# RWKV-6 recurrence and MLP on one core: round 0 loaded in rows of three steps, level 0 masked by AND, one MLP step moved between outputs and level products

## The chip, the cores and the metric

The kernel runs on one core of a Trainium2 chip. The core has a matrix engine (TensorE, called PE in the profile; its weight loads are listed apart as PEld), a vector engine (VectorE, DVE), a scalar engine (ScalarE, ACT), GpSimd (POOL), and a queue engine (SyncE, SP) that here only issues transfers. Each engine runs its own instructions in order and waits on semaphores for the others. Transfers run on 16 DMA engines; most are issued from SP's queue, a few from ACT's. The metric is the device time of one execution in microseconds (us). The times come from six executions, one of them with the profiler on.

## The reference

Four batches, eight heads, 768 steps, head size 48, all in float32. First a recurrence with a decaying state for each batch and head, then an MLP over the joined heads:

```python
for t in range(S):                       # S = 768, state is D x D per (batch, head), D = 48
    cur   = (u * k[t]) outer v[t]
    y[t]  = r[t] @ (state + cur)
    state = w[t][:, None] * state + k[t] outer v[t]
x  = y with heads joined                 # (4, 768, 384)
xn = (x - mean) / sqrt(var + 1e-6) * g_ln
out = x + relu(xn @ w_ch1) @ w_ch2       # 384 -> 1536 -> 384
```

## The kernel before

**Tiling.** The work is cut into 8 rounds, one for each batch and half of the sequence (384 steps). A round has two units of four heads each. A unit's `w`, `k`, `r` are loaded with one step per partition (`load`, line 122): three transfers of 128 steps for each tensor, in runs of 48 floats (192 bytes), into the tiles `nat_w`, `nat_k`, `nat_r`, where a head takes 64 columns, the last 16 of them zeros. `turned` (line 289) transposes them on PE, two heads at a time, in three blocks of 128 steps, into PSUM, and ACT copies the result into `wT` or `rkT`, so that head dimensions lie on partitions and steps along the free axis.

**The recurrence by levels.** Steps are grouped in chunks of 64. In a chunk the product between step s and a later step t carries the decays between them. This is done in six levels, lev = 0 to 5, for distances of 2^lev: `quads` (line 385) multiplies k by the odd halves of r for all chunks into PSUM (`a_ps`; 24 small products of each unit), `grow` (line 405, DVE) multiplies r and k in place by the decays of that level, and `keep` (line 422, DVE) copies from PSUM, by a mask, those elements of `a_ps` into the matrix `A` that belong to this level. `quads` of one level needs `grow` of the level before; `grow` must wait until `quads` has read. After the levels `ends`, `states`, `exchanged`, `own_outputs` and `outputs` form the chunk's state updates (`kn`, `kv`, `s`, `sx`) and the results y, and `own_term` adds the term with u. The sums of that term are made in rounds 0 and 1 by `product_sums` (line 359, small PE products with a selector, `own_ps`).

**The MLP.** `mlp(rnd)` (line 601) is a generator for one round: 12 steps of three products 128x128 by 128x384 (`h_ps`), then 12 steps of the second layer (`o_ps`). A step is six PE matmuls in the profile, since a float32 product is two passes there. The weights arrive as raw float32 and are rewritten once by ACT and DVE (`fetch`, `begin`, `shifted`, `added`, lines 217 to 273: four raw buffers, each begin asks for the next fetch).

**The order.** It is written out by hand: every engine runs its instructions in program order. First comes a prologue with round 0 (lines 695 to 777), in which `warm(n)` issues matmuls on zeros (tile `idle`) between the steps, and then a loop over rounds 1 to 8 and levels (lines 788 to 894). A slot of that loop (one round, one level) issues for an older round `states` in levels 0 and 1 and `outputs` in levels 2 and 3, then `quads`, `grow` and `keep` of the round itself, and then `fill` (line 658) mixes the other tasks (transposes for the next round and the like) with MLP steps, up to a count given by `UNTIL`. From round 3 on, the `y` products of `outputs` are thus followed at once by the `a_ps` products of `quads`:

```python
            elif old and lev < 2 * U:
                (states if lev < U else outputs)(old[lev % U])
            for q in now:
                if slot:
                    quads(q, lev)
```

PE's instructions come from memory as well: the profile lists the transfers of instructions as queues of their own (q8 and q14).

Of the kernel before, what the change touches and what calls it, by code (L numbers as in the profile page):

```python
# [12 lines left out]
I32 = mybir.dt.int32  # L13
# [39 lines left out]
def kernel(  # L53
# [68 lines left out]
    def load(q, which="wkr", eng=SP):  # L122
        for nm in which:
            for c in range(TT):
                eng.dma_start(
                    out=nat[nm][q % 2][:, c, :, 0:D],
                    in_=steps({"w": w, "k": k, "r": r}[nm], q, c),
                )

    def load_v(q, eng=SP):  # L130
        vn[q] = p4.tile([P, TT, NH, D], F32, tag="v", name=f"v{q}")
        for c in range(TT):
            eng.dma_start(out=vn[q][:, c], in_=steps(v, q, c))
# [9 lines left out]
            )  # L143


    load(0, "w", SPO)
    load(0, "r", ACT)
    load(0, "k", SPO)
    load(1, "wrk", SPO)

    sel = const.tile([P, H // 2, 2], F32, name="sel")
    POOL.memset(sel, 0.0)
# [12 lines left out]
    DVE.memset(eps, 1e-6)  # L165

    ACT.activation(out=const.tile([P, 1], F32, name="root"), in_=eps, func=AF.Sqrt)
    for nm in "wkr":
        for t in nat[nm]:
            POOL.memset(t[:, :, :, D:HP], 0.0)  # L170


    a_bufs = [const.tile([P, 2, U, NK, C], F32, name=f"A{i}") for i in range(2)]
# [5 lines left out]
    for lev in range(NLEV - 1):  # L179
        n = 1 << lev  # L180
        m = const.tile([P, C // n, n], I8, name=f"mask2_{lev}")
        POOL.memset(m, 1.0)
        for base, sign in ((0, 1), (n - 1, -1)):
            POOL.affine_select(
                out=m, in_=m, compare_op=ALU.is_ge, fill=0.0, base=base,
                pattern=[[-2 * n * sign, C // n], [0, n]], channel_multiplier=sign,
            )
        half = const.tile([P, C // 2], I8, name=f"mask{lev}")
        m = m.rearrange("p q n -> p (q n)")
        for i in range(2):  # L190
            rows = ds(C * i, C)
            POOL.tensor_copy(out=half[rows], in_=m[rows, ds(C // 2 * i, C // 2)])
        masks.append(half.rearrange("p (q n) -> p q n", n=n))

# [78 lines left out]
    def warm(n, tag="m"):  # L275

        while n > 0:
            m = min(n, RN // P)
            ps = (ps_m if tag == "m" else ps_t).tile([P, RN], F32, tag=tag, name="idle")
            PE.matmul(  # L280
                ps[:, 0 : m * P], nought.broadcast_to([P, P]), nought.broadcast_to([P, m * P]),
                start=True, stop=True,
            )
            n -= m
# [4 lines left out]
    def turned(q, nm, pr):  # L289
        a = st.setdefault(q, {})  # L290
        if pr == 0:
            if nm == "w":
                if q % U == 0:
                    st["w"] = p1.tile([P, U, W], F32, tag="w", name=f"wT{q // U}")
                a["w"] = st["w"][:, q % U]
            elif "rk" not in a:

                rk = a["rk"] = p4.tile([P, 2, W], F32, tag="rkT", name=f"rkT{q}")
                a["r"], a["k"] = rk[:, 0], rk[:, 1]
        ps = ps_t.tile([P, RN], F32, tag="t", name=f"{nm}_ps{q}_{pr}")  # L300
        for c in range(TT):
            PE.transpose(
                ps[:, ts(c, P)],
                nat[nm][q % 2][:, c, ts(pr, 2)].rearrange("p j d -> p (j d)"), ident,
            )
        ACT.copy(out=a[nm][:, ts(pr, RN)], in_=ps)
# [115 lines left out]
    def keep(rnd, lev):  # L422
        n = 1 << lev
        A, ps = a_bufs[rnd % 2], a_ps[rnd]
        if lev == NLEV - 1:
            for j in range(2):
                for i in range(2):
                    rows = ds(C * i, n)
                    late.append((A[rows, j, :, :, n:], ps[rows, j]))
        else:  # L430
            DVE.copy_predicated(
                out=A.rearrange("s j u k (q two n) -> s j (u k) q two n", two=2, n=n)[:, :, :, :, 1],
                mask=masks[lev][:, None, None].broadcast_to([P, 2, U * NK, C // (2 * n), n]),
                data=ps.rearrange("s j u k (q n) -> s j (u k) q n", n=n),
            )
        if lev == NLEV - 1:
            for q in units_of(rnd):

                a = st[q]
                a["rx"] = p2.tile([P, NK, C], F32, tag="rx", name=f"rx{q}")  # L440
                R = a["r"].rearrange("p (k i t) -> p k i t", i=2, t=C)
                for j in range(2):
                    late.append((a["rx"][ds(HP * (1 - j), HP)], R[ds(HP * j, HP), :, 1, :]))
# [232 lines left out]
    def each(f, *ranges):  # L676
        calls = [()]
        for r_ in ranges:
            calls = [c + (x,) for c in calls for x in r_]
        return [lambda c=c: f(*c) for c in calls]  # L680
# [17 lines left out]
    for nm in "wrk":  # L698
        run(each(turned, [u0], nm, pairs))
        warm(2)  # L700
    products(u0)
    quads(u0, 0)
    load(new[0], eng=SPO)
    grow(u0, 0)
    run(each(turned, [u1], "w", pairs))
    totals(0, DVE)
# [2 lines left out]
    for nm in "rk":  # L709
        run(each(turned, [u1], nm, pairs))  # L710
        warm(2)
    products(u1)
    quads(u1, 0)
    fetch(2)
# [11 lines left out]
    for lev in range(1, NLEV):  # L726
        quads(u0, lev)
        quads(u1, lev)
        run(ahead[2 * lev - 2 : 2 * lev] if lev < NLEV - 1 else [])
        if lev in (3, 4):  # L730
            begin()
        warm(3 if lev < NLEV - 1 else 0)
        for which in ("rk",) if lev < NLEV - 1 else "kr":
            for q in (u0, u1):
                grow(q, lev, which)
        keep(0, lev)
# [30 lines left out]
    quads(new[0], 0)  # L767
    quads(new[1], 0)
    warm(3)
    product_sums(new[0])  # L770
    warm(3)
    norm(0)
    begin()
    join()
# [13 lines left out]
    for rnd in range(1, NR + 1):  # L788
# [3 lines left out]
        for lev in range(NLEV):  # L792
            slot = (rnd - 1) * NLEV + lev
            if rnd == 2:

                for q in old if lev < 2 else []:
                    (states, outputs)[lev](q)
                if lev < 2:
                    mlp_step()
            elif old and lev < 2 * U:  # L800
                (states if lev < U else outputs)(old[lev % U])
            for q in now:
                if slot:
                    quads(q, lev)
# [8 lines left out]
            if rnd == 1:  # L813
                if lev < 2:
                    tasks += each(load, new, "kr"[lev], [SPO])
                if lev == 2:
                    SPO.dma_start(
                        out=u_bc,
                        in_=bass.AP(
                            tensor=u.tensor, offset=u.offset, ap=[[0, P], [D, H], [1, D]]  # L820
                        ),
                    )
                    tasks += each(load_v, now, [SPO])
                if lev == 3:
                    tasks += each(load_vx, now, [SPO])
                if lev == 1:
                    tasks += each(product_sums, now[1:])
                if lev in (4, 5):
                    own_term(now[lev - 4], POOL)
            if rnd == 2 and lev == 0:  # L830
# [96 lines left out]
```

## Time and profile before

| what | value |
|---|---|
| median of six executions | 591.06 us (589.32 to 594.54) |
| the profiled execution | 594.54 us, the slowest of the six |
| its span, first to last instruction | 592.5 us, so 2.04 us lie outside |
| granted TensorE clock, mean | 0.991 |
| PE busy | 569.9 us, 96% |
| DVE, ACT, POOL busy | 280.1, 194.8, 90.1 us |
| moved by DMA | 36.52 MB |

A share of busy time is an average over stages: the first 100 us (round 0, weights) have other limits than the rest, so each stage is read by itself, by its chain of waits and by the time in which PE has nothing running. "Issue" in the chain is time in which an engine stood still and waited for nothing that the profile shows. Groups such as `a_ps<-rkT` name the tile written and the tiles read.

### The profile page before, as it was taken

The page shows a single profiled execution, that of the slowest core. Times are in us where ns is not written, and L with a number is a line of the kernel's source. Part 1 is how long each engine was busy: PE and PEld are TensorE (multiplying, and loading weights), DVE is VectorE, ACT ScalarE, POOL GpSimd, SP SyncE. Part 2 cuts the span into 40 slices and gives each one's busy share as a digit, 9 for nine tenths or more (in the row PEclk, how much of TensorE's full clock was granted, in tenths as well). Part 3 has the DMA queues.
Part 4 walks back from the last instruction along what each step waited for, and adds up shares of the span by engine and source line. Part 5 has one row for each costly group of instructions (what it writes and reads, how often), then busy time and mean ns, then how long its engine had stood idle before and what let it go on. Part 6 is the DMA issues. An engine that isn't in the chain of part 4 may idle for free.

```text
span 592.5 us, 19009 instructions
## 1 busy us (share of the span) xinstructions
PE 569.9 (96%) x8538; PEld 382.1 (64%) x8538; DVE 280.1 (47%) x575; ACT 194.8 (33%) x426; POOL 90.1 (15%) x117
## 2 busy tenths in 40 slices
PE   8899989999999999889999899999999999999997
PEld 5676756666676766666666666667666666666554
DVE  4887999687282635424273335426245431130000
ACT  3576786313442224311433115321241015301200
POOL 6040011104430035000440007100230000000000
PEclk9998999999998999999999999999999999999999
DMA  9967885037304311340203402012000000000000
GB/s 146 189 167 167 206 232 120 12 80 137 72 16 99 65 34 23 67 81 24 54 5 74 83 14 55 2 32 59 16 1 3 14 29 2 1 15 27 0 14 27
DMA packets 120528, 36.52 MB, mean 62 GB/s; under 512 B 114176, under 2 KB 117376, under 8 KB 120448
## 3 DMA queue, kind: packets, MB, share of 16 engines
q1 hardware_dynamic: 118048, 35.01, 27.3%
q8 instruction: 67, 1.10, 0.8%
q10 hardware_dynamic: 2400, 0.30, 0.5%
q14 instruction: 13, 0.11, 0.1%
HBM read 28.51 MB, written 4.72 MB: 56 GB/s over the span
## 4 chain that ended last, share of the span: by engine, by line
PE 87%; ACT 5%; issue 2%; DVE 2%; DMA 2%; SPq 1%; ACTq 0%; DVEq 0%
PE o_ps L49 32%; PE h_ps L49 29%; PE a_ps L49 11%; PE y L49 4%; PE kv L49 2%; PE k_ps L49 2%; PE kn_ps L49 2%; PE w_ps L49 2%; PE xT_ps L49 1%; ACT rest L49 1%; PE r_ps L49 1%; ACT w_sb L49 1%; DMA nat_r<-in_r_dram 1%; PE idle L49 1%; DMA nat_k<-in_k_dram 1%
## 5 line engine op out<-in xcount | busy, mean ns | idle before, releaser
L49 PE MATMUL o_ps<-w_sb,h 128*128 128x384 f32 x576 | 200.7, 495 | 0.8 <-ACT h L49 0.8
L49 PE MATMUL h_ps<-xT,w_sb 128*128 128x384 f32 x576 | 198.2, 492 | 0.0
L49 PEld LDWEIGHTS o_ps<-w_sb,h 128*128 128x128 f32 x576 | 106.0, 193 | 63.1 <-issue 2.0
L49 PEld LDWEIGHTS h_ps<-xT,w_sb 128*128 128x128 f32 x576 | 105.7, 191 | 62.7 <-issue 0.6
L49 ACT ACTIVATE h<-h_ps 128x384 f32<-128x384 f32 x96 | 46.8, 488 | 143.2 <-PE h_ps L49 143.0
L49 PEld LDWEIGHTS a_ps<-rkT 48*64 48x64 f32 x4608 | 73.8, 135 | 23.8 <-issue 16.4
L49 DVE TENSOR_TENSOR rkT<-rkT,tot 128x768 f32<-128x768 f32 (+1 forms) x96 | 77.4, 844 | 21.3 <-PE a_ps L49 12.6
L49 PE MATMUL a_ps<-rkT 48*64 48x32 f32 x4608 | 79.0, 220 | 8.2 <-issue 8.2
L49 DVE TENSOR_TENSOR o<-o_ps,x 128x384 f32<-128x384 f32 x24 | 13.4, 558 | 136.9 <-PE o_ps L49 136.8
L49 POOL TENSOR_TENSOR vo<-v,own 128x576 f32<-128x576 f32 x16 | 19.6, 1225 | 301.3 <-DVE own L49 260.9
L49 DVE COPY_PREDICATED A<-mask,a_ps 128x768 f32<-128x768 int8 x40 | 53.4, 1334 | 0.0
L49 DVE SCALAR_TENSOR_TENSOR s<-s,decay,kv 128x48 f32<-128x48 f32 x160 | 29.3, 259 | 32.5 <-PE kv L49 32.5
L49 DVE TENSOR_TENSOR x<-y,vo 128x288 f32<-128x288 f32 x32 | 13.2, 453 | 53.4 <-PE y L49 53.3
L49 ACT ACTIVATE xT<-xT_ps,g_sb 128x384 f32<-128x384 f32 x24 | 13.6, 580 | 58.4 <-PE xT_ps L49 58.4
L49 ACT COPY rkT<-k_ps 128x384 f32<-128x384 f32 x32 | 14.4, 478 | 52.4 <-PE k_ps L49 52.4
L49 ACT COPY rkT<-r_ps 128x384 f32<-128x384 f32 x32 | 14.7, 478 | 32.4 <-PE r_ps L49 32.4
L49 DVE TENSOR_SCALAR w_sb<-w_sb 128x384 f32<-128x384 f32 (+1 forms) x48 | 19.3, 403 | 0.8
L49 DVE TENSOR_REDUCE own<-rk 128x12 f32<-128x576 f32 x12 | 9.0, 750 | 20.7 <-POOL rk L49 20.6
L49 ACT COPY wT<-w_ps 128x384 f32<-128x384 f32 x32 | 14.2, 479 | 12.6 <-PE w_ps L49 7.7
L49 ACT ACTIVATE rstd<-mv,eps 128x3 f32<-128x3 f32 x8 | 2.4, 297 | 48.2 <-DVE mv L49 48.0
L49 DVE TENSOR_TENSOR rkT<-rkT,wT 128x768 f32<-128x768 f32 x16 | 17.7, 1145 | 0.3
L49 PEld LDWEIGHTS r_ps<-ident,nat_r 128*128 128x128 f32 x96 | 11.7, 143 | 9.3 <-issue 3.5
(71 smaller groups left out, 512.8 us busy)
## 6 DMA issues: line engine op xcount, KB each, us to landing
raw<-in_moe_w_ch_dram SPq DMA_DIRECT2D x24, 384.0 KB, 4.5
nat_w<-in_w_dram SPq DMA_DIRECT2D x48, 96.0 KB, 2.9
nat_k<-in_k_dram SPq DMA_DIRECT2D x48, 96.0 KB, 2.9
v<-in_v_dram SPq DMA_DIRECT2D x48, 96.0 KB, 3.4
out_dram<-o SPq DMA_DIRECT2D x24, 192.0 KB, 1.9
nat_r<-in_r_dram SPq DMA_DIRECT2D x45, 96.0 KB, 2.9
vx<-v SPq DMA_DIRECT2D x28, 72.0 KB, 2.5
nat_r<-in_r_dram ACTq DMA_DIRECT2D x3, 96.0 KB, 4.0
```

The lines of the kernel that those rows point to most:

```text
L49: return lambda *args, **kw: self.tc.keep_in_program_order(f(*args, **kw))
```

## The change

1. The loads of round 0 (both units) are made by a new `load_rows`: one transfer for each tensor and unit, in which a partition holds three consecutive steps, 576 bytes in one run. `r` of both units goes by ACT's queue, the rest by SP's. The tile is then used flat, heads by 144 floats, with only its tail of 192 floats zeroed at the start; the 16 columns behind each head are zeroed by POOL later, when PE has read the unit.
2. For these two units `turned` no longer transposes: six products for each two heads (a window of 64 columns as weights, the identity as moving operand) write halves of the PSUM tile, and ACT's copy puts the steps back into order.
3. `keep` at level 0 is one DVE instruction that ANDs the PSUM values with a mask of ones and zeros (`bits0`, made once by POOL), instead of a predicated copy.
4. Round 1's first loads are issued in the order w, r, k instead of w, k, r.
5. In round 0, the weights' `begin` stands in levels 2 and 3 instead of 3 and 4.
6. `product_sums` of round 1's first unit, and a `warm(3)`, are taken out of the prologue; the sums are made in round 1, level 1, with those of the second unit.
7. From round 3 on, in levels 2 and 3, one MLP step is issued between `outputs` and `quads`. `fill` counts the steps done, so it issues one fewer.

```diff
+    def flat(nm, q):
+        return nat[nm][q % 2].rearrange("p c h d -> p (c h d)")
+
+    def load_rows(nm, q, eng):
+        b, f, g = units[q]
+        src = {"w": w, "k": k, "r": r}[nm]
+        eng.dma_start(
+            out=flat(nm, q)[:, 0 : NH * TT * D].rearrange("p (h x) -> p h x", h=NH),
+            in_=src[b, ts(g, NH), ds(f * RN, RN)].rearrange("h (p c) d -> p h (c d)", c=TT),
+        )
...
-    load(0, "w", SPO)
-    load(0, "r", ACT)
-    load(0, "k", SPO)
-    load(1, "wrk", SPO)
+    for q in range(U):
+        load_rows("w", q, SPO)
+        load_rows("r", q, ACT)
+        load_rows("k", q, SPO)
...
-    for nm in "wkr":
-        for t in nat[nm]:
-            POOL.memset(t[:, :, :, D:HP], 0.0)
+    for q in range(U):
+        for nm in "wrk":
+            POOL.memset(flat(nm, q)[:, NH * TT * D :], 0.0)
...
+    bits0 = const.tile([P, C // 2], I32, name="bits0")
+    POOL.tensor_scalar(
+        out=bits0, in0=masks[0].rearrange("p q n -> p (q n)"), scalar1=-1.0, scalar2=None,
+        op0=ALU.mult,
+    )
...
         ps = ps_t.tile([P, RN], F32, tag="t", name=f"{nm}_ps{q}_{pr}")
+        if q < U:
+            for c in range(TT):
+                for j in range(2):
+                    at = ((2 * pr + j) * TT + c) * D
+                    PE.matmul(
+                        ps[ds(HP * j, HP), ts(c, P)], flat(nm, q)[:, ds(at, HP)], ident,
+                        start=True, stop=True,
+                    )
+            ACT.copy(
+                out=a[nm][:, ts(pr, RN)].rearrange("p (m c) -> p m c", c=TT),
+                in_=ps.rearrange("p (c m) -> p m c", c=TT),
+            )
+            return
...
+        elif lev == 0:
+            DVE.tensor_tensor(
+                out=A.bitcast(I32).rearrange("s j u k (q two) -> s j (u k) q two", two=2)[..., 1],
+                in0=ps.bitcast(I32).rearrange("s j u k q -> s j (u k) q"),
+                in1=bits0[:, None, None].broadcast_to([P, 2, U * NK, C // 2]),
+                op=ALU.bitwise_and,
+            )
...
+    for nm in "wrk":
+        POOL.memset(nat[nm][0][:, :, :, D:HP], 0.0)
     products(u0)
     quads(u0, 0)
-    load(new[0], eng=SPO)
+    load(new[0], "wrk", SPO)
...
+    for nm in "wrk":
+        POOL.memset(nat[nm][1][:, :, :, D:HP], 0.0)
...
-        if lev in (3, 4):
+        if lev in (2, 3):
             begin()
...
     warm(3)
-    product_sums(new[0])
-    warm(3)
     norm(0)
...
                 (states if lev < U else outputs)(old[lev % U])
+                if lev >= U and now:
+                    mlp_step()
...
                 if lev == 1:
-                    tasks += each(product_sums, now[1:])
+                    tasks += each(product_sums, now)
```

## The prediction

> **What bounds the kernel now.** I read the page first, then the chain of waits in order of time, then the clock by stretches, then the timeline of the first 20 us.
>
> ```profile
> PE 569.9 (96%) x8538; PEld 382.1 (64%) x8538; DVE 280.1 (47%) x575; ACT 194.8 (33%) x426; POOL 90.1 (15%) x117
> q8 instruction: 67, 1.10, 0.8%
> L49 PE MATMUL a_ps<-rkT 48*64 48x32 f32 x4608 | 79.0, 220 | 8.2 <-issue 8.2
> ```
>
> PE is the bound from about 100 us on, so a change pays there only if it fills PE's holes or shortens its work. The third line gives the holes: before `a_ps` PE stood 8.2 us for "issue", for nothing that the profile shows. The second hints at what it is: 67 transfers of instructions, 1.10 MB, so 16 KB each; PE's 17076 recorded instructions over 67 make one transfer for about 255 instructions. The chain shows one hole in round 4, level 2:
>
> ```profile
> 245.30 1.55 PE y L49 x96
> 246.84 0.92 PE a_ps L49 x64
> 247.76 1.49 issue
> 249.25 0.67 PE a_ps L49 x29
> 249.92 0.48 PE k_ps L49 x3
> 250.40 3.34 PE o_ps L49 x6
> 253.74 0.62 PE k_ps L49 x3
> 254.36 1.94 PE o_ps L49 x6
> ```
>
> The hole lies inside `a_ps`, where no data is awaited. 96 `y` and 96 `a_ps` matmuls with a weight load each are 384 instructions in 2.9 us, more than one transfer's worth, while an MLP step has 12 in 1.94 us. I read it as instructions running out. The chain has five such holes at the ten places where `outputs` meets `quads` in rounds 3 to 7: 1.06 us at 183.74, 1.49 at 247.76, 1.56 at 263.73, 1.83 at 332.26, 1.04 at 455.60, in sum 6.98. After the second, an `o_ps` step takes 3.34 instead of 1.94:
>
> ```profile
> 250.00:254.00 4.00, 4.00 (x12) 2.31 (x12) 1.82 (x2) 0.48 (x1) 0.00 (x0) 0.60 0.20 41
> 254.00:258.00 4.00, 4.00 (x16) 2.57 (x15) 0.00 (x0) 0.96 (x2) 0.00 (x0) 0.97 0.41 74
> ```
>
> The sixth figure after the stretch is the granted clock: 0.60 after the hole, then full. After the hole at 183.74 it is the same (3.63 for the step). So two holes cost 1.40 and 1.69 more: 3.09.
>
> The prologue is a chain through several engines. PE's part in round 0 (timeline), and the way to the MLP (chain):
>
> ```profile
> 10.91 0.87 PE L49 MATMUL w_ps<-ident,nat_w 128*128 128x128 f32 x6
> 11.62 0.60 PE L49 MATMUL idle<-nought 128*128 128x256 f32 x2
> 12.06 1.47 PE L49 MATMUL own_ps<-sel,ruk 128*128 128x2 f32 x12
> ```
>
> ```profile
> 48.43 0.84 PE idle L49 x2
> 49.27 1.25 PE own_ps L49 x12
> 50.54 0.17 ACT own L49
> 50.71 0.20 ACT rstd L49
> 51.15 1.27 DVE xn L49 x3
> 54.37 2.92 PE h_ps L49 x6
> ```
>
> **The change, part by part** (times against the profiled execution, 594.54 us, span 592.5).
>
> *The MLP step between outputs and quads.* No work is added. Of ten places each gets 1.94 us of big matmuls between two bursts of 192 instructions, so 256 instructions in a row then last 1.94 plus 122 small matmuls at 0.0155 (1.5/96), 3.8 us, where the hole at 247.76 ended 128 matmuls of 2.0 us and the wait of 1.49: 3.5 us. That suffices by a little. Gain 6.98 + 3.09 = 10.1 if all holes go, 0 if they only move; I take 10.1, since all of the five lie in bursts that are now cut. What it costs: every change between small and large tiles shows in the chain. An `o_ps` step right after `a_ps` takes 2.13 instead of 1.94, and `a_ps` right after `o_ps` 1.53 instead of 1.39 after `y`. Each place gets one more of each, 0.33, so ten add 3.3. Net gain 6.8. No wait is added on PE: the step reads weights and `h` made long before. `fill` loses the step again, so the transposes in these slots stand a little closer; ACT's copies for them (0.48) have 1.94 us of cover each.
>
> A rule speaks against this part: the Trainium skill, "Runtime: NRT & Kernel Launch", section on instruction fetch mechanics, says that fetching runs ahead and that crossing a 16 KiB boundary is mostly hidden, with room for 2048 instructions on PE. By it the holes would have another cause, the 10.1 would be 0 and this part would lose 3.3. The row of 8.2 us for "issue" is nearer.
>
> *The sums out of the prologue.* `rstd` on ACT stood behind `own`, which waited for `own_ps`, 1.25, behind a `warm(3)`, 0.84. ACT's copies of k end at 47.47, so `rstd` comes 3 us sooner; DVE is free from 47.48 (it had 3.46 idle), `xn` ends near 49.3 and the first `h_ps` near 51.5 instead of 54.2: 2.7. The 1.25 us of products come back in level 1, and from 67 us on the chain goes through ACT and DVE, which keep the earlier start in part. I take 2.0, ends 0 (the weights' arrival takes over: ACT waits once for `raw`, 1.6) and 2.7. The clock also halves at this spot (`h_ps` 2.92 for 1.94); I take 0.5 for that, ends 0 and 1.
>
> *Round 0.* For u0 and u1 there are 12 calls of `turned`. Each was three matmuls (0.87/2 = 0.43 for one), and is now six products of two passes each, 12 passes. No row shows 128 rows by 64 columns. If two halves run side by side, as the four quarters do in `y`, a pair of passes takes one transpose's 0.11 (0.33/3): 0.66. If passes run one by one as in `own_ps` (1.47/12 = 0.122): 1.47. I take 0.70, because `y` (16 ns a matmul, where 48 columns at the rate of `o_ps`, 0.323/384, take 40) is nearest in shape. On both sides of a `warm` the tile shape now changes: 0.33 for each tensor and unit. So a tensor costs 1.40 + 0.33 instead of 0.87, 0.86 more. For u1 nothing hides it: PE runs without a break from 10.07 to 14.47 and then waits 0.26 for k's load; 3 × 0.86 − 0.26 = 2.3. For u0 the loads come first: PE waited until 6.25 for the last of w, and ACT's table load ended at 7.01. The new loads carry the same 1.77 MB in 6 transfers of 576-byte runs instead of 18 of 192; ACT's queue spends 1.1 us on two issues where it had 1.65 on three, so ACT is ready some 0.5 earlier, w at 5 instead of 6.25. From there 3 × 0.86 less these 1.25 leaves 1.3 later. Together 3.6; later loads and instructions find a less crowded DMA (share over 1.3 from 4 to 7 and 17 to 22 us), which may take the holes at 22.54 (1.25) and 28.02 (0.56): I take 0.3 off, 3.3. Ends: 0.66 and no cost of shapes, less the 1.25 and both holes, is 12 × 0.23 − 0.26 − 1.25 − 1.8 = −0.6; 1.47 instead of 0.70 is 9.2 more, 12.5.
>
> The DMA page of the skill ("DMA: Bandwidth & Descriptors", specifications) puts full rate at 512 bytes and up, which would make these loads a gain. In the trace 192-byte runs already moved 200 and 209 GB/s between 2 and 4 us. By either the loads land before PE asks for u1.
>
> *Level 0 by AND.* Eight predicated copies of 768 elements (1.9 us in rounds 0 and 1, 0.96 at best) become eight ANDs; nearest is the level-0 product `rkT` with the same stride, 0.96. Bounds −0.9 to +0.9 each. Six lie under PE-bound stages (DVE 47% busy). In round 0 PE fills level 1 itself, in round 1 DVE is 91% busy between 66 and 98 us: I take 0.5 for both.
>
> *At nothing:* POOL's memsets (two took 0.45; six more) and `bits0`: masks ended at 12.1, the next POOL work was at 29.66, waiting for v; PE's first transposes of round 1 now wait for those memsets too, the first of which needs only u0's products, done some 8 us before; without that cover a transpose group would slip by 0.23. ACT's reordering copies (0.43; the stride-2 weight copies took 0.45 to 0.65) stay below the 0.70 of PE. SP: 14 fewer issues in front, r before k for round 1, all needed after 24 us; without that lead, one load is 2.9 us. The `begin` at level 2 puts 1.75 us of ACT before the k copies of level 3, where ACT was idle 2.1; its raw tile is asked for earlier on SP; if late, ACT slips by at most 1.6, its one wait for `raw`.
>
> *Sum:* −6.8 − 2.5 + 3.3 − 0.5 = −6.5. The profiled execution is the slowest of the six, 3.5 above the median; one hole with its slow clock costs about 3, so the others may have one fewer. Taken from the median in full it is 584.6; with 1.5 of the gain not there to be had, 586.0.
>
> **Rivals.**
> - *The holes move.* The boundaries come at every 256 instructions and shift with the 216 new ones of round 0 (144 passes with loads, 288, for 36 matmuls with loads, 72). The two `outputs` of round 2 (hole of 1.40 at 117.08) remain a burst of 384. Against it: a cut burst lasts 3.8 us. If half the holes stay: −1.7 − 2.5 + 3.3 − 0.5 = −1.4, 589.7, no change. 0.20.
> - *Slower: products one by one.* Place: the first 20 us, PE. The forecast breaks even at 6.5/12 = 0.54 above 0.70, 1.24 for a call or 0.104 a pass, and is 0.5% slower at 1.49, 0.124 a pass. `own_ps` has 0.122; with weight loads in the open (0.14 + 0.11) a call takes 3.0: 12 × 2.3 = 28 more, 612. For it: this tile shape is not in the trace. Against: `y` and `kv` overlap. 0.12, at 594 to 612.
> - *Round 0 costs nothing.* The lower ends together: −6.8 − 3.7 − 0.6 − 0.9 = −12: 579. 0.13.
>
> **How the numbers follow.** The forecast has 0.55, with its own range 582 to 589.5; its upper end is within 0.5%. A measurement tells about 0.5% from no change, 588.1 to 594.0. Faster: nine tenths of the forecast and the last rival, 0.62. Same: the moved holes and the rest, 0.26. Slower: 0.12. The range runs from 579.0 to 592.5: below lies part of the last rival, above the slow one.
>
> **What would show it.** Right: in rounds 3 to 7 an `o_ps` step of 2.13 between `y` and `a_ps`, no "issue" there, and the clock at full after 100 us; `h_ps` about 1 us earlier or more against the end of round 0; `w_ps` pairs of 0.7 in the first 20 us, and `a_ps` of u1 some 3.5 later than 16.42. Wrong: holes at other places of the chain, product calls of 1.3 us and more, or an MLP start delayed by `raw`.

## The result, and the profile after

The changed kernel takes 588.96 us (median of 36 executions, 585.45 to 592.24), the kernel before 592.33 (median of 73, 587.21 to 599.61). The ratio is 0.9949, with a 95% interval of 0.9934 to 0.9963: 2.2 to 3.9 us faster. The forecast was 586.0, against the 591.06 of the first six executions. The sign is right and the time lies in the range, but the gain is smaller than the 5.1 us forecast. Two later sets of executions of the same kernel gave 0.9929 [0.9897, 0.9961] and 0.9924 [0.9891, 0.9957].

The profiled execution takes 589.3 us, close to the median, with a span of 587.3. From the page of the kernel after, the engines' busy time, the instruction queue, the clock by slices, and two groups:

```profile
PE 576.1 (98%) x8644; PEld 387.1 (66%) x8644; DVE 272.7 (46%) x575; ACT 195.1 (33%) x426; POOL 91.1 (16%) x124
PEclk9997799999999999999999999999999999999999
q8 instruction: 68, 1.11, 0.8%
L49 PE MATMUL a_ps<-rkT 48*64 48x32 f32 x4608 | 77.9, 221 | 0.0
L49 DVE COPY_PREDICATED A<-mask,a_ps 128x768 f32<-128x768 int8 x32 | 38.4, 1199 | 0.0
```

The idle time before `a_ps` is now 0.0, where it was 8.2. The step does what the prediction says of it. The chain of waits of the kernel after in round 4, level 2 (start, duration, engine, tile), where the hole of 1.49 stood:

```profile
245.24 1.55 PE y L49 x96
246.78 2.13 PE o_ps L49 x6
248.91 1.53 PE a_ps L49 x96
```

The price is also the forecast one, 2.13 and 1.53. But the clock's digits show the other side: it falls to 7 in slices 4 and 5, between 44 and 73 us, where the lowest digit of the kernel before was 8. The same from the view of busy time by stretches, kernel after (from the left: PE, PEld, DVE, ACT and POOL busy; then the granted clock, the DMA share and GB/s):

```profile
47.00:66.00 19.00, 18.97 (x256) 14.48 (x255) 18.14 (x38) 11.14 (x25) 0.00 (x0) 0.77 0.97 201
52.00:72.00 20.00, 19.97 (x171) 14.32 (x170) 16.94 (x34) 10.72 (x24) 0.00 (x0) 0.79 0.80 165
100.00:400.00 300.00, 298.46 (x5062) 202.65 (x5061) 145.35 (x298) 91.33 (x204) 61.42 (x58) 1.00 0.26 54
```

PE is busy through the whole of both early stretches, but at 0.77 and 0.79 of its clock (before: 0.91 in each). From 100 to 400 us the clock is 1.00 and PE stands still for 1.54 us (before: 8.42, at 0.99).

So two points divide the span. The first `o_ps` product comes at 95.5 us instead of 92.5, 3.0 later; from there to the last instruction it takes 491.7 instead of 500.0, 8.3 less. The forecast had +0.3 (3.3 − 2.5 − 0.5) for the first part and −6.8 for the second. The prologue is thus 2.7 worse than forecast and the rest 1.5 better.

The chain of waits of the kernel after shows where the early part goes:

```profile
45.98 0.33 ACT rkT L49
46.30 0.04 issue
46.35 1.37 PE k_ps L49 x6
47.72 2.72 PE a_ps L49 x96
50.44 1.58 PE idle L49 x2
...
53.89 1.94 PE h_ps L49 x6
...
60.36 1.53 PE a_ps L49 x96
61.89 3.58 PE own_ps L49 x24
65.47 4.05 PE h_ps L49 x6
```

`a_ps` takes 2.72 instead of 1.53 and `idle` 1.58 instead of 0.84: half clock, from 46.6 to 53.4 us. This first stretch stands ahead of the sums: it begins just behind a wait of PE, 1.52 us up to 46.35, for ACT's copy into `rkT`. The next one, 63.6 to 70.5, begins in the 24 `own_ps` products that the change has put in a row in round 1, level 1, and makes an `h_ps` step 4.05 instead of 1.94.

### The profile page after: what moved, and what is told of

Read it like the earlier page. It is cut to its first block, busy times and chain, and to the rows that moved or that the text cites. A ratio compares the mean times of both kernels' runs of the same rounds, so it can differ in the third digit from the quotient of the medians.

```text
span 587.3 us, 19224 instructions
## 1 busy us (share of the span) xinstructions
PE 576.1 (98%) x8644; PEld 387.1 (66%) x8644; DVE 272.7 (46%) x575; ACT 195.1 (33%) x426; POOL 91.1 (16%) x124
## 4 chain that ended last, share of the span: by engine, by line
PE 92%; ACT 3%; DVE 3%; issue 1%; DVEq 0%; ACTq 0%
PE o_ps L49 32%; PE h_ps L49 31%; PE a_ps L49 12%; PE y L49 4%; PE k_ps L49 2%; PE w_ps L49 2%; PE idle L49 2%; PE kv L49 2%; PE r_ps L49 2%; PE kn_ps L49 2%; PE xT_ps L49 2%; DVE w_sb L49 1%; ACT rest L49 1%; PE own_ps L49 1%; DVE s L49 1%
## 5 line engine op out<-in xcount | busy, mean ns | idle before, releaser
L49 PEld LDWEIGHTS o_ps<-w_sb,h 128*128 128x128 f32 x576 | 104.5, 190 | 62.3 <-ACT h L49 1.9
L49 DVE TENSOR_TENSOR rkT<-rkT,tot 128x768 f32<-128x768 f32 (+1 forms) x96 | 75.7, 831 | 40.3 <-issue 26.0
L49 DVE COPY_PREDICATED A<-mask,a_ps 128x768 f32<-128x768 int8 x32 | 38.4, 1199 | 0.0
L49 ACT ACTIVATE xT<-xT_ps,g_sb 128x384 f32<-128x384 f32 x24 | 13.7, 580 | 56.3 <-PE xT_ps L49 56.2
L49 PE MATMUL k_ps<-ident,nat_k 128*128 128x128 f32 (+1 forms) x132 | 16.2, 285 | 1.8 <-ACT rkT L49 1.8
```

What stands on the lines that cost most here:

```text
L49: return lambda *args, **kw: self.tc.keep_in_program_order(f(*args, **kw))
```

## The experiments

The changed kernel is two things in one: edits that fall almost wholly into the first 100 us (only the AND recurs in later rounds), and a step after them. The theories to be told apart:

1. **Holes from instruction fetch**: a hole stands where a whole block of 256 instructions lies in one burst of small products. The step cuts the burst. Its rival is *the holes move*: they shift with the instruction count, and the step is worth little.
2. **The loss of the prologue**: it comes from round 0's rows and products (their own time, or the 216 instructions that they add), or from the sums in their new place, with the clock that falls there.

Kernels were run in five sets, each with the kernel before beside it on the same chip. The median of the kernel before was 594.20, 593.81, 592.44, 595.88 and 593.34 in the five, and single executions of one kernel spread over 3 to 9 us. So ratios are compared across sets, times only within a set, and differences of less than about 2 us are not settled. All edits are against the kernel before or the changed kernel, as said.

### The step alone (e1, f1; sets 1 and 4)

To the kernel before, only the step is added:

```diff
                 (states if lev < U else outputs)(old[lev % U])
+                if lev >= U and now:
+                    mlp_step()
```

> The kernel before with the MLP step between outputs and quads alone. Theory A (the step is worth its forecast and more, what comes ahead of 100 us took part of it back): the five holes inside a_ps and both slow-clock stretches after them are gone, the stretch from the first o_ps to the end falls from 498.4 us to about 490, time 0.986 to 0.990 of before. Rival B (the step is worth less than forecast, because without the profiler the holes are fewer): the holes are gone in the profile, but the time is 0.994 to 0.997. Rival C (the holes only move): holes at other places of the chain after 100 us, 0.997 to 1.003.

> The kernel with the MLP step alone, again, beside the next two on one chip: 0.985 to 0.989, first o_ps near 92.

Measured: 586.16 us, ratio 0.9857 [0.9818, 0.9895], and 587.32, 0.9890 [0.9845, 0.9936]: 8.0 and 8.6 us faster within their sets, more than the whole change. In the profiles the first `o_ps` comes at 92.0 and 92.9 (before 92.5), and the rest takes 492.3 and 492.1 instead of 500.0. The chain of the step alone (e1), where the hole of 1.06 at 183.74 stood, and the clock in the stretch that is 0.91 before and 0.79 after:

```profile
180.46 1.54 PE y L49 x88
182.01 2.13 PE o_ps L49 x6
184.14 1.53 PE a_ps L49 x96
```

```profile
52.00:72.00 20.00, 19.66 (x269) 13.72 (x268) 18.90 (x36) 15.59 (x35) 0.00 (x0) 1.00 0.92 206
```

So the step is worth at least what was forecast (−6.8), and the other edits together cost 2 to 5 us on top of it (0.9949, 0.9929 and 0.9924 for all edits against 0.9857 and 0.9890).

### The changed kernel without the step (e2, set 1)

```diff
                 (states if lev < U else outputs)(old[lev % U])
-                if lev >= U and now:
-                    mlp_step()
```

> The changed kernel without the MLP step between outputs and quads; all else of the change stays. Theory A: holes inside a_ps return at some of the ten places, first o_ps near 97 as in the changed kernel, so the rest of the change costs about 3 us: 1.003 to 1.007 of before. Rival B: the rest of the change is worth nothing or gains a little, as forecast with 3.3 - 2.5 - 0.5 = +0.3: 0.998 to 1.002.

Measured: 589.14 us, 0.9908 [0.9873, 0.9943]: as fast as the changed kernel with the step (0.9949, 0.9929, 0.9924). Two holes are left of five, the chain of this kernel shows:

```profile
242.90 1.27 PE a_ps L49 x86
244.18 1.14 issue
...
324.82 1.14 issue
```

Its part behind the first `o_ps` takes 491.7 us, as with the step. On the changed kernel, then, the step gains nothing that can be measured: what is left of holes and slow clock (2.3 of "issue" and one stretch of 3.4 us at half clock, so 1.7) costs about what ten changes of shape cost (3.3). That the holes are fewer because round 0's new instructions move the boundaries is the reading of the count in the next section. The gain of 8 that the step has on the kernel before is a gain against the place where its boundaries happen to lie. This is the rival of the moving holes, true for the kernel without the step.

### Boundaries shifted by 128 instructions (e8, set 2)

To the kernel before, 32 small products on zeros are added in the prologue. A float32 product is two passes with a load each, so they are 128 PE instructions, half a block. No step is added.

```diff
     warm(8)
+    pad = [ps_m.tile([P, RN], F32, tag="m", name=f"pad{i}") for i in range(2)]
+    for i in range(8):
+        for a in range(2):
+            for c in range(2):
+                PE.matmul(
+                    pad[c][ds(C * (a ^ c), C), 0:D],
+                    nought[ds(C * c, C)].broadcast_to([C, C]),
+                    nought[ds(C * c, C)].broadcast_to([C, D]), start=True, stop=True,
+                )
```

> The kernel before with 32 small products on zeros behind the first warm: 128 more PE instructions and nothing else. Theory F (a hole stands where a whole block of 256 instructions lies in one burst of y and a_ps): the boundaries shift by half a block, so the holes at the five places of before are gone, and holes stand at the other five: round 3 level 3, round 5 level 2, round 6 levels 2 and 3, round 7 level 3; the one in round 2's outputs (117.08) goes as well. Rival G (the holes belong to their place, by what data or transfers do there): the same five places as before. Time within 0.995 to 1.005 of before by either.

Measured: 591.56 us, 0.9950 [0.9915, 0.9984]. All five old holes are gone, and so is the one at 117 us. Three new ones stand in the chain of this kernel (rounds 5, 6 and 7):

```profile
315.61 1.54 issue
317.15 0.43 PE a_ps L49 x5
...
396.88 1.15 PE a_ps L49 x80
398.03 1.51 issue
...
464.17 1.18 issue
```

I counted PE's instructions from the start in blocks of 256. By this count a whole block lies inside the burst of 368 or 384 instructions at just five of the kernel before's ten places, and these are the five with holes. Shifted by 128, another five places hold a whole block: the three seen, and two in round 3, level 3, and round 6, level 2, where no hole came. In e2, by the same count, four places hold a whole block, and two of them had a hole. So at these ten places a whole block in the burst is needed for a hole, in all three kernels, but doesn't always bring one. (Round 0 has holes too, in shorter bursts.) Doing more work (the products on zeros) thus even made the kernel a little faster, by chance of the count.

The traces allow a sharper count, with PE's semaphore instructions taken in. By it all 74 waits of PE's products of 0.2 us and more that the 20 profiles put down to "issue" end at one place of a block of 256, at its instruction 192 or 193 counted from the first one recorded: the holes stand at block boundaries. The count also parts the spared places from the others: where a hole came, the block that ends at it begins 44 to 119 instructions behind the burst's start, at the four spared places 12, 17, 42 and 43. No run was made to test that gap, so it stays an observation.

The Trainium skill, "Runtime: NRT & Kernel Launch", section "Instruction fetch mechanics", gives the same unit, blocks of 16 KiB and 256 instructions, and calls the crossing mostly hidden. The first agrees with the count here; the second does not hold in these bursts, where a crossing left PE idle for 1.0 to 1.8 us.

### The old loads with all other edits (e3, set 1)

The changed kernel with round 0's loads, transposes and memsets of the kernel before:

```diff
-    for q in range(U):
-        load_rows("w", q, SPO)
-        load_rows("r", q, ACT)
-        load_rows("k", q, SPO)
+    load(0, "w", SPO)
+    load(0, "r", ACT)
+    load(0, "k", SPO)
+    load(1, "wrk", SPO)
...
-        if q < U:
+        if False:
```

> The changed kernel with round 0's loads and transposes as before (AND, begin, sums and MLP step as changed). Theory A (the loss before 100 us comes from the slow clock after the own_ps products that now follow a_ps in round 1, level 1): u1's level 0 starts near 16.4 instead of 19.8, but holes in the levels of round 0 (1.25 and 0.56 before) give part back; first o_ps 95 to 97, 0.992 to 0.995 of before. Rival D (the loss comes from the products of 64 columns in round 0): first o_ps 3.4 earlier, near 94, 0.988 to 0.991.

Measured: 588.15 us, 0.9878 [0.9833, 0.9923], so 2.0 slower than the step alone in the same set by the medians and 0.5 by the means, which these spreads don't settle. By the forecast it should have been 3.0 faster (sums −2.5, AND −0.5). In the profile the first `h_ps` comes at 49.17, 3.95 earlier than in e1, and the first `o_ps` at 89.6, 2.4 earlier; but this execution (583.23) is the fastest of its six, so it doesn't show what the median lost; the clock that is recorded for each execution does, further below. What the profile does show is the clock behind the sums (stretches of 4 us):

```profile
56.00:60.00 4.00, 4.00 (x117) 3.96 (x109) 3.86 (x9) 1.35 (x4) 0.00 (x0) 1.00 0.94 275
60.00:64.00 4.00, 4.00 (x11) 2.22 (x11) 3.79 (x7) 0.34 (x2) 0.00 (x0) 0.57 1.04 199
```

The 24 `own_ps` end at 60.1; the clock in the next 4 us is 0.57.

### The sums back in the prologue (e4, set 1)

```diff
     warm(3)
+    product_sums(new[0])
+    warm(3)
     norm(0)
...
                 if lev == 1:
-                    tasks += each(product_sums, now)
+                    tasks += each(product_sums, now[1:])
```

> The changed kernel with the sums of round 1's first unit and the warm(3) back in the prologue. Theory A: the half-clock stretch from 63.6 to 70.5 us is gone, first o_ps 94 to 96 instead of 97.3, 0.989 to 0.993 of before. Rival D: rstd waits for own_ps again, which costs 2.0 us as forecast, first o_ps near 99, 0.997 to 1.000.

Measured: 589.00 us, 0.9928 [0.9893, 0.9963], the same as the changed kernel. In the profiles the first `h_ps` is at 56.36 against 53.73, but 2.1 of these 2.6 us stand already at the first `kv` (39.18 against 37.06), ahead of the sums; and the first `o_ps` is at 95.4 against 95.5. So nothing of the 2.5 us is left at the first `o_ps`; but the changed kernel stands at half clock for 13.7 us before it, this one for 3.4.

### The sums apart from each other (e7 and f4, sets 2 and 4; g2, set 5)

If the row of 24 products does the harm, two rows of 12 with MLP steps between should not. Unit 1's sums go into level 1 and unit 2's into level 2, mixed with the other tasks. In e7 and f4 this is added to e3 (old loads), in g2 to the changed kernel.

```diff
-                if lev == 1:
-                    tasks += each(product_sums, now)
...
-                tasks += mixed([begin] * BEGINS[lev], [join] * JOINS[lev], ahead[:n])
+                sums = each(product_sums, now[lev - 1 : lev]) if lev in (1, 2) else []
+                tasks += mixed(sums, [begin] * BEGINS[lev], [join] * JOINS[lev], ahead[:n])
```

> The changed kernel with round 0's old loads and transposes, and with the sums of round 1's two units taken apart: one in level 1 and one in level 2, each between MLP steps instead of together behind a_ps. If small products in a row slow the clock, the slow stretch at 60.3 of the kernel with old loads is gone and the first o_ps comes 1 us earlier than 89.57: span about 580, ratio 0.980 to 0.986. If the slow stretch has another cause it stays, 0.986 to 0.990.

> Old loads, step, AND, begin and sums taken apart, again: 0.981 to 0.985, below the kernel with the step alone by 0.003 to 0.005, if AND, begin and the sums are worth their 2.5 to 3 us once the sums no longer stand in a row; level with it if they are worth nothing.

> The changed kernel with the sums of the two units taken apart (one in level 1, one in level 2, between MLP steps). If the row of small products cost the gain of the moved sums: 0.003 to 0.005 below the changed kernel, first o_ps 2 to 4 us earlier and no slow clock at 60 to 71 us. If the loss lies in round 0 alone: within 0.002 of it.

With the old loads: 582.99 us, 0.9816 [0.9775, 0.9858], and 584.74, 0.9832 [0.9788, 0.9876]. f4 is 2.6 faster than the step alone in the same set (f1), near the 3.0 forecast for sums and AND together, and e7 and f4 have the lowest ratios of all kernels run. The first `o_ps` comes at 88.4 and 88.5, about 4 earlier than with the step alone. With the new loads: 587.21, 0.9895 [0.9861, 0.9928], 1.9 faster than the changed kernel in the same set (g1; 2.4 by the means), first `o_ps` at 92.2 against 99.2. Of these 7 us, 2.6 stand already at the first `h_ps`, ahead of the sums, since g1's profile has two holes in round 0.

The chain of the changed kernel run again (g1), and of the same with the sums apart (g2), round 1:

```profile
65.45 1.53 PE a_ps L49 x96
66.98 2.77 PE own_ps L49 x24
69.75 3.75 PE h_ps L49 x6
```

```profile
64.02 1.94 PE h_ps L49 x6
...
66.28 1.23 PE own_ps L49 x12
67.52 2.04 PE h_ps L49 x6
...
76.43 1.25 PE own_ps L49 x12
```

The `h_ps` step behind the 24 takes 3.75, behind 12 it takes 2.04. Of the profiled executions with 24 in a row behind `a_ps`, four of five show half clock that begins in them or right behind them (after, its two repeats, e3; not e2); of those with the sums apart (e7, f4, g2 and the two below) none does. With 12 there and 12 in the prologue it is mixed: four of ten (e4, e8, e11, f2) have a stretch of 3.4 us right behind the 12, the others (before, e1, e6, e9, f1, f3) have none. The edit changes two things at once, the length of the row and its place behind `a_ps`; these runs don't part them.

One profile is one execution, but the mean clock is on record for every execution. The share that is missing to full clock, times the span, estimates what half clock took; the rest is the time without it. (A stretch at the very end counts too, up to 1 us in the profiles.) The mean of that loss is 4.4 us over the 63 executions with the step and 24 in a row (after, e5, g1, e3), 2.7 over the 71 with 12 and 12 (e1, e4, e6, e9, e11, f1, f2, f3), and 1.9 over the 30 with the sums apart (e7, e10, e12, f4, g2): between the first and the last 2.5, with a 95% interval of 1.7 to 3.2 by resampling the executions. Means of each set against the kernel before in the same set, in us (each good to about 1 without clock, 2 for the clock):

| kernel | sums | time without half clock | half clock |
|---|---|---|---|
| e1, f1: step alone | 12 and 12 | −3.9, −2.5 | −3.4, −4.8 |
| e6, f2: step and rows | 12 and 12 | +0.8, +0.6 | −2.5, −4.6 |
| e4: all but the sums | 12 and 12 | −1.0 | −3.0 |
| e5, g1: changed kernel | 24 in a row | −2.9, −3.4 | −1.5, −0.8 |
| e2: changed kernel, no step | 24 in a row | −3.9 | −0.6 |
| g2: changed kernel | apart | −4.6 | −2.0 |
| e3: old loads | 24 in a row | −6.1 | −0.7 |
| e7, f4: old loads | apart | −6.1, −5.7 | −4.6, −5.1 |

Without half clock, e3 is as fast as e7 and f4 and some 2 us faster than e1; what it loses is clock.

### The changed kernel again (e5 and g1, sets 2 and 5), and the step and the rows alone (e6 and f2, sets 2 and 4)

e5 and g1 are the changed kernel without an edit. In e6 and f2 the AND, the new place of `begin`, the sums and the load order are taken back, so that the step and round 0's rows and products are left:

```diff
-        elif lev == 0:
...
-    load(new[0], "wrk", SPO)
+    load(new[0], eng=SPO)
...
-        if lev in (2, 3):
+        if lev in (3, 4):
...
     warm(3)
+    product_sums(new[0])
+    warm(3)
     norm(0)
...
-                    tasks += each(product_sums, now)
+                    tasks += each(product_sums, now[1:])
```

> The changed kernel once more, beside the others on one chip. Its ratio to before is 0.9949 so far. If the two slow-clock stretches of its profile (6.8 us each, before 71 us) belong to it and are no accident, they stand again between 44 and 71 us, and u1's level 0 starts near 19.8, the first h_ps near 53.7, the first o_ps near 95.5. If they are chance, fewer stretches and a first o_ps near 92 to 93.

> The changed kernel, beside the next one on one chip: 0.992 to 0.996 of before, a slow-clock stretch behind the 24 own_ps products near 64 to 67 us.

> The kernel before with the MLP step and round 0's new loads and products, but with the predicated copy, begin, sums and load order as before (bits0 is made and not used). Against the kernel with the step alone (584.3 us span, first o_ps 91.96). Theory A (round 0's products cost more than the forecast 3.3, because they bring PE to the MLP later and at a slow clock): u1's level 0 3.4 later than 16.45, first o_ps 95 to 98, ratio 0.992 to 0.997. Rival E (they cost what was forecast and the levels' holes give part back): first o_ps 93 to 94, 0.987 to 0.990.

> Step and round 0's loads and products, again. If PE's own time is all (3.4 us): 0.0055 to 0.006 above the kernel with the step alone. If holes at shifted boundaries and slow clock double it: 0.009 to 0.012 above.

Measured: e5 589.11 us, 0.9929; g1 589.07, 0.9924; e6 591.86, 0.9966 [0.9934, 0.9997]; f2 590.45, 0.9934 [0.9899, 0.9968]. f2 is 3.1 slower than f1 in the same set: the rows cost what was forecast for them (+3.3). By ratio, in different sets, e6 lies 6.5 above e1; f2 and the pair e10 and e12 below don't bear that out. The AND with the sums and `begin` is worth 2.7 by e5 against e6, but f2's ratio equals that of the changed kernel; between 0 and 2.7 it is open.

The profiles also show a hole in round 0 that the kernel after had not. The chain of e6:

```profile
31.64 0.46 PE a_ps L49 x18
32.10 1.09 issue
33.20 1.36 PE a_ps L49 x78
34.56 1.21 PE w_ps L49 x6
35.77 1.28 PE idle L49 x2
37.05 2.15 PE a_ps L49 x96
```

After it the clock halves, as it does after two of the later holes of the kernel before: `w_ps` 1.21 for 0.81, `idle` 1.28, `a_ps` 2.15. e5 and g1 have two such holes (1.09 and 1.70, between 31 and 38 us), and their first `o_ps` is at 99.0 and 99.2 rather than 95.5; f2 has only 0.27 there. So at the same place the same kernel has the hole in one execution and not in another. The wait for `rkT` ahead of `k_ps`, too, is not the sums': it is 1.5 us in after, e2, e4, e5, e12, f3, g1 and g2, and half clock begins within 1.8 us behind it in all but e4 and e5; where it is 0.7 to 1.2 (e1, e3, e8, e10, f1, f4) none begins. The executions with the two holes, 592.88 and 593.02, are the second slowest of 12 and the slowest of 8. The first profile of the kernel after, without them, lies at the median.

### Is it the instructions or the time of the rows? (e11 and f3, sets 3 and 4; e9, set 3)

e11 and f3 are e1 with 216 PE instructions of products on zeros (54 of e8's products) behind `warm(8)`: the boundaries of the rows without their work. e9 is e1 with `warm(5)` for `warm(2)` at three places of the source in round 0: more products on zeros, which delay u1's level 0 by 2.6 us.

```diff
     warm(8)
+    for i in range(54):
...
```

```diff
         run(each(turned, [u0], nm, pairs))
-        warm(2)
+        warm(5)
```

> The kernel with the MLP step alone, with 54 small products on zeros behind the first warm: 216 more PE instructions, as many as round 0's products bring, in about 1 us. Theory A': round 0 starts 0 to 1 us later, but the boundaries of its instruction blocks stand as in the changed kernel, so holes and slow clock stand in the levels and states of round 0 (20 to 50 us), first o_ps 94 to 97. Rival H: the instructions do nothing, first o_ps 92 to 93, 0.985 to 0.988.

> Step and 216 more instructions without the work. If the shift of boundaries costs by itself: 0.003 to 0.006 above the kernel with the step alone, with a hole near 32 us and slow clock after it in the profile. If not: within 0.002 of it.

> The kernel with the MLP step alone (584.3 us span, u1's level 0 at 16.45, first o_ps at 91.96, 0.9857 of before), with warm(5) instead of warm(2) at the six places of round 0: about 3.4 us more of PE, in large matmuls, with 24 instructions. Theory A' (round 0's products cost their own time, and the rest comes from holes at the shifted instruction boundaries and the slow clock after them): level 0 of u1 near 19.8, first o_ps 95 to 96, no slow clock before 60 us, 0.990 to 0.993. Rival H (any delay of PE in round 0 is paid twice, because it shifts what ACT, DVE and DMA do): first o_ps 98 to 100, 0.995 to 0.999.

Measured: e11 585.48 us, 0.9897 [0.9874, 0.9920], and f3 586.16, 0.9855 [0.9809, 0.9901]: no slower than the step alone. Their profiles have holes at 32.3 (1.37) and 32.8 (0.82), the slow clock behind them, and a first `o_ps` 2.8 and 3.5 later than their e1 and f1; but both profiled executions are the slowest of their six. The holes of round 0 thus cost when they come, and don't come often enough to move the median. e9: 590.36 us, 0.9973 [0.9953, 0.9992]; first `o_ps` at 95.0 against 92.0 in e1. Its delay of 2.6 arrives in full there, and the median is 4.2 above e1's, which ran in another set. So time lost on PE in round 0 is not caught up later, which is what the forecast took for u1, and it is the time of the rows that costs.

### One more cut, in round 2 (e10 and e12, set 3)

Round 2's two `outputs` stand in a row, with a hole of 1.40 in the kernel before. An MLP step goes between them; e10 is e7 with this, e12 the changed kernel with the sums apart and this.

```diff
                     (states, outputs)[lev](q)
-                if lev < 2:
-                    mlp_step()
+                    if lev == 1 or q == old[-1]:
+                        mlp_step()
```

> The kernel with old loads and sums taken apart (582.6 us span, 0.9816), with one of round 2's MLP steps moved between the two outputs there. By theory F the hole of 1.49 at 113.3 and the slow clock after it (1.7) go, for one more pair of changes of tile shape (0.33): 0.976 to 0.981. If the hole is due to something else it stays and the ratio is 0.981 to 0.985.

> The changed kernel with the sums taken apart and round 2's outputs cut by an MLP step: it differs from the kernel with old loads, sums apart and cut outputs by round 0's loads and products alone. Theory A': first o_ps 3.4 us later plus holes and slow clock of round 0, 4 to 7 us in all, ratio 0.007 to 0.012 higher. Rival E (the products cost what was forecast at most): 2 to 3.5 us, 0.003 to 0.006 higher.

Measured: e10 583.94 us, 0.9875 [0.9846, 0.9903]; e12 587.01, 0.9929 [0.9904, 0.9955]. e10's hole is gone, but PE now waits 1.27 us at 122.24 for DVE's `xn`, and two transfers stand in the chain ahead of that, so one wait has taken the place of another. The chain of e10:

```profile
117.47 4.03 DMA v<-in_v_dram
...
121.58 2.15 DMA vx<-v
```

No gain over e7 or g2 can be told. The pair gives the price of the rows once more, 3.1.

## Why the prediction was right and wrong

**The MLP step between outputs and quads: right on the kernel before, and its mechanism too.** Forecast −6.8, in the profile −8.3, and 8.0 and 8.6 in time where it is the only edit (without half clock −3.9 and −2.5, where holes and changes of shape gave 3.3 − 6.98 = −3.7; for the clock −3.4 and −4.8, where the forecast was −3.1). The mechanism was instruction fetch, as read from the 67 transfers: the holes' places follow the count of 256 (e8, and all 74 waits), and cutting the burst ends them. What the prediction didn't see is that the tail's 8 us are also had without the step: on the changed kernel, e2 keeps just two holes. The prediction adds its terms as if each held on the changed kernel, and there this one measures about 0. *The holes move* was put as a rival to the gain; holes do move, but the ten cut bursts hold none of more than 0.4 us in the profile of the kernel after, and the two ways of losing holes don't add.

**Round 0: right in size.** A call of `turned` takes 0.73 (24 passes in 1.46) where 0.70 was taken, so two halves run side by side at 0.061 a pass, and the slower rival (0.122) is out. From the timeline of the kernel after, PE in round 0:

```profile
12.30 1.53 PE L49 MATMUL w_ps<-ident,nat_w 128*64 128x128 f32 x24
13.76 0.70 PE L49 MATMUL idle<-nought 128*128 128x256 f32 x2
14.30 1.39 PE L49 MATMUL own_ps<-sel,ruk 128*128 128x2 f32 x12
```

u1's level 0 begins at 19.81 instead of 16.42, 3.4 later (forecast some 3.5), and the two pairs of runs give +3.1 in time (forecast +3.3). The loads came early, as said: 228 GB/s over the first 15 us, where it was 145, and 342 to 353 between 3 and 6 us, where the 192-byte runs had 155 to 209. (SP has 11 fewer issues in front, 4 for 15, and not the 14 of the prediction; nothing hung on it.)

**The sums out of the prologue: the time right, the clock wrong, and this is the step that failed.** The prediction had 2.0 for the earlier start and 0.5 for the clock, both as gains. The first came: without half clock the changed kernel (e5, g1) lies 1.9 and 2.4 below e4, which differs by the sums alone. The second went the other way. The prediction priced the products that "come back in level 1" at their own 1.25 us, and left out what follows them: half clock behind the 24 in a row, one or two stretches of 3.4 us in the profiles. The whole forecast for the profiled execution, −6.5, was −2.9 without the clock (−6.98 for holes, +3.3 for shapes, −2.0 for the sums, +3.3 for round 0, −0.5 for the AND) and −3.6 for the clock (−3.09 and −0.5). Measured were −2.9 and −3.4 without it, but only −1.5 and −0.8 for it: the shortfall of some 2 to 3 us is all clock. That the row in this place is the cause is shown by moving it alone: with the sums apart and the old loads (e7 and f4 against e3, in three sets) the time without half clock stays within 0.4 us and the clock's part goes from −0.7 to −4.6 and −5.1. On the changed kernel (g2 against g1) each of the two falls by 1.2. That the clock is the way from cause to cost is what the mean clock of all executions says, and the profiles show the place; no run held the clock fixed. Part of the changed kernel's slow clock has another place, behind the wait ahead of `k_ps` at 45 us; the prediction didn't see it either, and no run takes it away alone.

**AND at level 0: right where it can be seen.** The first AND takes 0.95 where the copy took 1.9; its 0.5 us can't be told from 0 here. (Without half clock e4 is 1.6 to 1.8 below e6 and f2, which were run in other sets and differ by the AND, `begin` and the load order together.)

**From the profiled execution to the median: also wrong.** The sum was −6.5 and the profiles give −5.2: 2.7 lost ahead of the first `o_ps`, 1.5 gained behind it. The forecast then stood 2.0 below 594.54 − 6.5, because the profiled execution was the slowest of six. But that execution is 2.2 above the median of 73, while the changed kernel's is only 0.3 above its own. Taking most of the surplus off again left 586.0; of the 3.0 us between 586.0 and 588.96, 1.7 come from there and 1.3 from the sum.

**What stays open:** what in the row (its length, its shape, its place behind `a_ps`) brings half clock, and why not in e2's profile; whether the 44 instructions that part the spared places of e8 and e2 from the others are a bound; why the same kernel has a hole near 32 us in one execution and not in another.

## What to carry to other kernels

Count a long burst of small PE instructions against the block of 256: where a whole block can fall into one burst, put large products between, and judge the edit with the boundaries moved as well, since any edit early in the program moves all of them and can change the time by chance: e2's part behind the first `o_ps` is 8 us shorter than before, with no edit aimed at its holes. Price a moved row of small products with what stands behind it, not by its own time: spread among large products the same sums kept the gain that they lost to half clock in a row. The version to keep is the step, the AND, the early `begin` and the sums apart, with the old loads (e7, f4): 0.9816 and 0.9832, faster than both kernels.

## What the runs showed of the hardware

- The holes in PE's work stand at one place of a block of 256 instructions: 74 of 74 "issue" waits of PE of 0.2 us and more in the 20 profiles.
- A hole of 1.0 to 1.9 us is sometimes followed by half clock for 3.4 us or two or three times that (11 of 32 holes, within 2 us): 1.09 us idle in e6, then 3.4 us in which `a_ps` takes 2.15 for 1.53. The row of 24 products of two columns is followed by the same without any hole. The Trainium skill, "TensorE: Matmul & The Clock Gate", section "What's actually happening", gives a window of about 3.4 us, which fits the lengths here (3.41, 6.83 and 10.24 us); the idle time of a whole window that it names for the fall isn't in these traces, where PE's longest wait is 1.94 us.
- Two products of 128 rows by 64 columns into the two halves of a PSUM tile overlap: 0.061 us a pass, about half of a 128x128 transpose's 0.11 or of the 0.122 in `own_ps`.
- 128 instructions of useless work early in the program moved all five holes of the later rounds, and the kernel got no slower for it.
